# Attention tokens in transposed order, batch stores of 16 partitions, and another order of the first loads

## The chip, the cores and the metric

The kernel runs on one core of a Trainium2 chip. A core has five engines with a queue each: TensorE (PE, with weight loads shown as PEld), VectorE (DVE), ScalarE (ACT), GpSimd (POOL) and SyncE (SP, which here only issues transfers). Each queue runs in order; engines wait for each other by semaphores. Transfers between device memory and the on-chip memory run on 16 DMA engines and are issued from the queues of SP, ACT and POOL. The metric is the device time of one execution in microseconds (us).

## The reference

Two blocks follow each other. The inputs are q, k and v of 8 batches, 8 heads, 576 tokens, 64 numbers each, float32.

```
k_p = k.reshape(B, H, Sp, 8, D).mean(axis=3)          # 576 keys -> 72 pooled keys; v_p the same
scores = scale * q @ k_p^T ; attn = softmax(scores)
x = (attn @ v_p) as (B, S, H*D)                       # 8 x 576 x 512
s = x @ w_gate ; top_idx = the 128 tokens of a batch with the largest s
out = x ; out[top_idx] += sigmoid(s[top_idx]) * (relu(x[top_idx] @ w1) @ w2)   # 512 -> 1024 -> 512
```

Every token of x is written to the output; 128 tokens of each batch are then read back, sent through the two matrices w1 and w2, and written again.

## The kernel before

The work of a batch is cut into six *steps* of 96 tokens; there are 48 steps, numbered a = 0 to 47, and 14 more for what is left after the last attention. Two steps make a *unit* u.

The attention. k and q of a batch come as [128 partitions = 8 heads x 16 groups of 36 tokens]; v comes as [72 pooled rows] in two halves of four heads, each half as a transfer of 64 partitions and one of 8. `pool_k`, `k_trans` and `q_trans` build transposed operands, `pool_v` sums v over the pool of eight and multiplies it with the gate's weights, `gate_v` reduces that product to one column. `scores(u)` (L209) makes 32 matmuls into the PSUM tile pS and then one exponential on ACT (L220) for two steps at once: 72 partitions of 1536 numbers. The six token groups t and sixteen token groups g of a step lie in pS as (t g); the exponential writes them as (g t), so that consecutive results are six numbers apart. `attend(a)` (L226) makes the eight heads' matmuls into pA; `norm(a)` reads pA with two small ACT instructions (zall L244, ss L245) and two DVE instructions (rz L247, xs L248). pS and pA each have one buffer: `scores(u+1)` waits for the exponential of u, `attend(a+1)` for `norm(a)`.

The stores. After every second step ACT's queue issues a store of 96 partitions, two tokens each (L270), three per batch.

The second block of batch b is spread over later steps by a list of jobs: `at(a, slot, job)` puts a job into step a, slot 0 to 3. With e = 6(b+1), the first step of the next batch: `score` on DVE and POOL at e-1; `row_bcast` in two halves at e, slots 2 and 3: three transposes on PE into the tile pM, a copy by ACT (sr, L295), three more into the same pM, a copy. pM has one buffer, so PE's second three wait for ACT's first copy. Then come `count` and `one_hot` (DVE, steps e+2 to e+5), `gather` at e+6 (POOL issues the indirect read of 128 rows of the output, xr, L331, which waits for the stores of the batch), `x_trans` at e+7 slot 3 (PE, L346), `hidden` (L358) and `finish` (pF, L368, and POOL's indirect write, L374). So step e of a batch holds the first step of attention of the next batch, `row_bcast` of this one, `gather` of the one before it and part of `finish` of the one before that, and step e+1 ends with `x_trans`. I call the stretch from the second half of `attend(e)` to `x_trans` in e+1 the *boundary* at step e; boundaries with all their parts lie at steps 12, 18, 24, 30, 36 and 42.

The order of a step is written out: slot 0, `attend(a)`, `norm(a)`, slot 1, on even steps `scores(u+1)` and `q_trans(u+2)`, slots 2 and 3. PE, DVE, ACT and POOL run their parts in just that order.

The loads. SP issues k(b+2), q(b+2) and the two halves of v(b+2) during batch b, w1 at the start and w2 in step 3. v has three buffers (L101), k and q two. Load q(b+2) waits for the last `q_trans` of batch b, which stands in the first step of batch b+1.

One thing is not in the text of the kernel: the transfers that SP and ACT issue share eight completion semaphores, which the built program hands out in turn, over both queues together. Each transfer waits, at its place in its queue, until the transfer that had its semaphore before, eight transfers earlier, has landed. The list of waits in the built program names these.

At the end a check of all normalizers (L459 to L463) decides whether a second, general path is run; it isn't run here.

Of the kernel before, what the change touches and what calls it, by code (L numbers as in the profile page):

```python
# [7 lines left out]
FT = mybir.dt.float32  # L8
BF = mybir.dt.bfloat16
I32 = mybir.dt.int32  # L10
AF = mybir.ActivationFunctionType
# [37 lines left out]
def direct_path(ctx, tc, q, k, v, moe_w_gate, moe_w1, moe_w2, moe_capacity, out, flag):  # L49
# [49 lines left out]
        nc.sync.dma_start(out=QR[b], in_=q[b].rearrange("h (g t) d -> (h g) t d", g=G))  # L99

    def load_v(b, g, eng):  # L101
        x = work.tile([SP, HG, POOLW, D], FT, name="vraw", bufs=3)
        VR[b, g] = x
        src = v[b, HG * g : HG * (g + 1)].rearrange("h (p t) d -> p h (t d)", t=POOLW)
        for lo, hi in ((0, 64), (64, SP)):
            eng.dma_start(out=x[lo:hi].rearrange("p h t d -> p h (t d)"), in_=src[lo:hi])

    load_k(0)
    load_v(0, 0, nc.scalar)
    load_q(0)  # L110
    load_v(0, 1, nc.scalar)

# [2 lines left out]
                        in_=bass.AP(tensor=moe_w_gate.tensor, offset=moe_w_gate.offset, ap=[[0, SP], [1, DM]]))  # L117
    eps = const.tile([C, 1], FT)
    nc.vector.memset(eps, 1e-9 * POOLW)
    diff = const.tile([128, 128], FT)  # L120
    nc.gpsimd.iota(diff, pattern=[[1, 128]], base=0, channel_multiplier=-1,
                   allow_small_or_imprecise_dtypes=True)
# [21 lines left out]
    def constants():  # L144
        nc.vector.tensor_scalar(ident, diff, 0.0, None, op0=OP.is_equal)
        nc.vector.tensor_scalar(before, diff[:C, :C], 0.0, None, op0=OP.is_lt)
        nc.vector.memset(ones, 1.0)

        hi = const.tile([C, 1], FT, name="hi")
        stepped = const.tile([C, CT], FT, name="stepped")  # L150
        for t in range(CT):
            nc.vector.tensor_scalar(stepped[:, t : t + 1], part, float(G * (t + 1)), None, op0=OP.is_ge)
        nc.vector.tensor_reduce(out=hi, in_=stepped, axis=AX.X, op=OP.add)
        lo = const.tile([C, 1], FT, name="lo")
        nc.vector.scalar_tensor_tensor(lo, hi, -float(G), part, op0=OP.mult, op1=OP.add)
        nc.vector.tensor_scalar(lo, lo, float(NC), None, op0=OP.mult)
        nc.vector.tensor_scalar(hi, hi, float(NC * G), None, op0=OP.mult)
        for a in auxb:
            nc.vector.tensor_scalar(a[:, :, 0], chunk0, lo, None, op0=OP.add)
            nc.vector.tensor_scalar(a[:, :, 1], chunk0, 0.0, hi, op0=OP.mult, op1=OP.add)  # L160

# [2 lines left out]
    def pool_k(b, eng):  # L166
        x = KR[b].rearrange("p (r t) d -> p r t d", r=R)
        KS[b] = work.tile([128, R, D], FT, name="ks", bufs=1)
        eng.tensor_tensor(out=x[:, :, 0:2, :], in0=x[:, :, 0:2, :], in1=x[:, :, 2:4, :], op=OP.add)  # L169
        eng.tensor_tensor(out=KS[b], in0=x[:, :, 0, :], in1=x[:, :, 1, :], op=OP.add)  # L170
# [11 lines left out]
    def pool_v(b, g, eng):  # L182
        x = VR[b, g]
        VP[b] = vps[b % 2]
        h = slice(HG * g, HG * g + HG)
        eng.tensor_tensor(out=x[:, :, 0:4, :], in0=x[:, :, 0:4, :], in1=x[:, :, 4:8, :], op=OP.add)  # L186
        eng.tensor_tensor(out=x[:, :, 0:2, :], in0=x[:, :, 0:2, :], in1=x[:, :, 2:4, :], op=OP.add)  # L187
        eng.tensor_tensor(out=VP[b][:, h, 0:D], in0=x[:, :, 0, :], in1=x[:, :, 1, :], op=OP.add)

        eng.tensor_tensor(out=x[:, :, 2, :], in0=VP[b][:, h, 0:D], in1=wg[:, h, :], op=OP.mult)  # L190

    def gate_v(b, g):
        h = slice(HG * g, HG * g + HG)
        nc.vector.tensor_reduce(out=VP[b][:, h, D + 1], in_=VR[b, g][:, :, 2, :], axis=AX.X, op=OP.add)  # L194
# [5 lines left out]
    def q_trans(u):  # L200

        b, th = divmod(u, NTH)
        QT[u] = work.tile([128, 2, 2, CT, 32], FT, name="qt")
        nc.vector.transpose(  # L204
            out=QT[u].rearrange("p cc j t c -> p t (cc j) c"),
            in_=QR[b].rearrange("p (t c) d -> p t (c d)", c=NC)[:, :, 2 * D * th : 2 * D * (th + 1)].rearrange(
                "p t (a e) -> p t a e", e=32))

    def scores(u):  # L209
        b = u // NTH  # L210
        p = psum.tile([SP, 4, 4, 128], FT, name="pS")
        for s in range(2):
            for j in range(2):
                for i in range(4):
                    r = slice(32 * i, 32 * i + 32)
                    nc.tensor.matmul(p[:, i, 2 * s : 2 * s + 2, 0:C], KT[b][r, j, s, :],  # L216
                                     QT[u][r, :, j, :, G * s : G * s + G],
                                     start=(j == 0), stop=(j == 1))
        ET[u] = work.tile([SP, H * 2, G, CT], FT, name="et")
        nc.scalar.activation(ET[u].rearrange("p n g t -> p n t g"),  # L220
                             p.rearrange("p i n x -> p (i n) x")[:, :, 0:C].rearrange("p n (t g) -> p n t g", g=G),
                             AF.Exp, scale=exp_scale)

    PA = {}

    def attend(a):  # L226
        u, cc = divmod(a, 2)
        b = u // NTH
        p = psum.tile([C, 2, 512], FT, name="pA")
        for h in range(H):  # L230
            g, n = divmod(h, HG)
            nc.tensor.matmul(p[:, g, E * n : E * n + E], ET[u][:, 2 * h + cc].rearrange("p g t -> p (g t)"),  # L232
                             VP[b][:, h, :], start=True, stop=True)
        PA[a] = p[:, :, 0 : HG * E].rearrange("p g (n d) -> p g n d", d=E)

# [23 lines left out]
    def others(ins, b, kinds):  # L259
        for o in range(B):  # L260

            if o != b and not (kinds[-1] is gath and b == B - 1 and o == B - 2):
                for s in kinds:
                    for x in s.get(o, ()):
                        tc.declare_no_dep(ins.ins, x.ins, reason="rows of another batch")

    def store_x(u):
        b, th = divmod(u, NTH)
        c = slice(2 * th, 2 * th + 2)
        i = nc.scalar.dma_start(out=out[b].rearrange("(p c) d -> p c d", c=NC)[:, c, :], in_=XS[b][:, c, :])  # L270
        others(i, b, (scat, gath))
        store.setdefault(b, []).append(i)

    def score(b):
        nc.vector.tensor_tensor(out=SS[b], in0=SS[b], in1=RZ[b], op=OP.mult)
# [107 lines left out]
    def at(a, slot, *job):  # L383
        jobs.setdefault((a, slot), []).append(job)


    for u in range(NU):
        at(2 * u + 2, 1, store_x, u)
    for b in range(B):
        e = NC * (b + 1)  # L390
        last = b == B - 1
        at(e - 1, 3, score, b)
        at(e, 2, row_bcast, b, 0)
        at(e, 3, row_bcast, b, 1)
        for c in range(NC):
            at(e + (1 if last else (2, 2, 3, 3, 4, 5)[c]), 3, count, b, c)
        at(e + (2 if last else 5), 3, one_hot, b)
        at(e + (5 if last else 6), 3 if last else 1, gather, b)
        at(e + 7, 1, gate, b)
        at(e + 7, 3, x_trans, b)  # L400
        for n, f in enumerate((0, 1, 2, 3, 4, 5, 8, 6, 7, 9, 10, 11, 12, 13, 14, 15)):
            c = (0, 0, 1, 1, 2, 2, 2, 3, 3, 3, 4, 4, 4, 5, 5, 5)[n]
            slot = (1, 2, 1, 2, 1, 2, 2, 1, 2, 2, 1, 2, 2, 1, 2, 2)[n]
            at(e + 8 + c, slot, *((hidden, b, f) if f < 8 else (finish, b, f - 8)))
        if b + 1 < B:
            a = NC * b
            at(a, 0, pool_k, b + 1, nc.gpsimd)
            at(a + 1, 3, pool_v, b + 1, 0, nc.gpsimd)
            at(a + 2, 1, k_trans, b + 1)
            at(a + 3, 3, pool_v, b + 1, 1, nc.gpsimd)  # L410
            at(a + 4, 3, gate_v, b + 1, 0)
            at(a + 5, 3, gate_v, b + 1, 1)
        if b + 2 < B:
            at(a, 1, load_k, b + 2)
            at(a + 1, 1, load_q, b + 2)
            at(a + 2, 1, load_v, b + 2, 0, nc.sync)
            at(a + 4, 3, load_v, b + 2, 1, nc.sync)

    def run(a, slot):
        for f, *x in jobs.get((a, slot), ()):  # L420
            f(*x)

    pool_k(0, nc.vector)
    pool_v(0, 0, nc.gpsimd)
    k_trans(0)
    q_trans(0)
    scores(0)
    pool_v(0, 1, nc.vector)
    gate_v(0, 1)
    gate_v(0, 0)  # L430
    q_trans(1)
    load_k(1)
    for g in range(2):
        load_v(1, g, nc.sync)
    load_q(1)
    constants()
    nc.sync.dma_start(out=w1, in_=moe_w1.rearrange("(a p) f -> p a f", p=128))
    at(3, 1, lambda: nc.sync.dma_start(out=w2, in_=moe_w2.rearrange("(a p) n -> p a n", p=128)))

    for a in range(NCH + 14):  # L440
        run(a, 0)
        if a < NCH:
            attend(a)
            norm(a)
        run(a, 1)
        u = a // 2
        if a % 2 == 0 and u + 1 < NU:
            scores(u + 1)
            if u + 2 < NU:
                q_trans(u + 2)  # L450
        run(a, 2)
        run(a, 3)
# [367 lines left out]
```

## Time and profile before

| | |
|---|---|
| median of three executions | 365.19 us (364.87 to 366.78) |
| the profiled execution: time, span | 366.8 us, 364.9 us |
| mean granted TensorE clock | 0.865 of full speed |
| PE matmul busy | 275.2 us (75%) |
| DVE busy | 177.9 us (49%) |
| POOL busy | 134.5 us (37%) |
| ACT busy | 104.9 us (29%) |
| bytes moved | 46.75 MB, mean 128 GB/s |

The span is from the first to the last instruction of the profiled execution. An engine's busy time is the sum of its instructions' durations; issuing a transfer and waiting are not in it. The chain that ended last is followed back from the last instruction, at each step to what released it; PE has 44% of it, DVE 22%, transfers 16%, ACT 6%.

### The profile page before, as it was taken

How to read it: one execution, taken by the hardware profiler on the slowest of the kernel's cores; microseconds unless marked ns; L12 is line 12 of the kernel's file. 1: busy time of each engine (PE TensorE's matmuls, PEld its weight loads, DVE VectorE, ACT ScalarE, POOL GpSimd, SP SyncE). 2: the span in 40 equal slices, each digit the busy share in tenths (PEclk: the TensorE clock that was granted, in tenths of full speed). 3: DMA queues.
4: the chain of work that ended last, by engine and by line, in shares of the span. 5: the costliest groups of instructions: out<-in, count | busy, mean ns of one | idle time of the engine just before them, and what ended most of it. 6: DMA issues, size and time to landing. Idle time of an engine off the chain costs nothing.

```text
span 364.9 us, 5869 instructions
## 1 busy us (share of the span) xinstructions
PE 275.2 (75%) x2306; PEld 216.3 (59%) x2306; DVE 177.9 (49%) x524; ACT 104.9 (29%) x169; POOL 134.5 (37%) x156
## 2 busy tenths in 40 slices
PE   0303777788658988969778989698879889989890
PEld 0203666576637875767557755686668669556650
DVE  3249244158423752594429723946294627563001
ACT  0310333422240444324314441432343244110100
POOL 1177501950359015660647064805390210121101
PEclk9999766655565998988999998969996999999996
DMA  7932999961781178306661686031121113210101
GB/s 272 268 58 54 372 353 304 321 140 44 208 249 50 44 195 247 94 15 151 224 158 31 141 295 142 0 110 46 38 65 43 46 29 93 66 60 11 48 0 39
DMA packets 12952, 46.75 MB, mean 128 GB/s; under 512 B 1324, under 2 KB 1324, under 8 KB 10868
## 3 DMA queue, kind: packets, MB, share of 16 engines
q1 hardware_dynamic: 8240, 31.33, 29.4%
q10 hardware_dynamic: 3396, 10.77, 10.0%
q0 software_dynamic: 1280, 4.20, 4.2%
q8 instruction: 20, 0.33, 0.4%
q14 instruction: 16, 0.13, 0.1%
HBM read 34.75 MB, written 11.53 MB: 127 GB/s over the span
## 4 chain that ended last, share of the span: by engine, by line
PE 44%; DVE 22%; DMA 16%; ACT 6%; issue 5%; POOL 4%; ACTq 1%; DVEq 0%; SPq 0%; POOLq 0%
PE pA L232 14%; PE pM L358 10%; PE pS L216 8%; DMA xr<-out_dram,idx 8%; PE pF L368 8%; DMA vraw<-in_v_dram 7%; DVE xs L248 4%; ACT et L220 4%; DVE cmp L309 3%; POOL kraw L169 2%; DVE cmp L305 2%; DVE qt L204 2%; DVE cmp L307 2%; DVE oh L316 2%; DVE kh L175 2%
## 5 line engine op out<-in xcount | busy, mean ns | idle before, releaser
L232 PE MATMUL pA<-vp,et 72*96 72x66 f32 x768 | 90.8, 281 | 47.7 <-DVE vp L194 24.6
L232 PEld LDWEIGHTS pA<-vp,et 72*96 72x96 f32 x768 | 86.3, 195 | 59.0 <-issue 28.5
L220 ACT ACTIVATE et<-pS 72x1536 f32<-72x1536 f32 x24 | 70.7, 2947 | 61.9 <-PE pS L216 61.9
L358 PE MATMUL pM<-xg,w 128*128 128x128 f32 x512 | 71.3, 292 | 2.8 <-ACT xg L348 1.5
L358 PEld LDWEIGHTS pM<-xg,w 128*128 128x128 f32 x512 | 65.0, 203 | 8.7 <-issue 5.0
L368 PE MATMUL pF<-w,ht 128*128 128x512 f32 x128 | 65.2, 632 | 0.0
L247 DVE RECIPROCAL rz<-zall 96x8 f32<-96x8 f32 x48 | 9.5, 198 | 113.9 <-ACT zall L244 112.4
L216 PE MATMUL pS<-qt,kt 32*72 32x192 f32 x768 | 52.4, 428 | 12.0 <-DVE qt L204 12.0
L216 PEld LDWEIGHTS pS<-qt,kt 32*72 32x72 f32 x768 | 36.5, 184 | 19.4 <-DVE qt L204 12.0
L281 POOL CAST auxb<-sc 96x6 bf16<-96x6 f32 x8 | 1.6, 199 | 121.0 <-DVE sc L277 105.0
L186 POOL TENSOR_TENSOR vraw<-vraw 72x1024 f32<-72x1024 f32 x15 | 35.5, 2368 | 19.7 <-DMA vraw<-in_v_dram 19.6
L244 ACT ACTIVATE zall<-pA,eps 96x8 f32<-96x8 f32 x48 | 12.2, 254 | 93.8 <-PE pA L232 93.8
L248 DVE TENSOR_TENSOR xs<-pA,rz 96x512 f32<-96x512 f32 x48 | 33.0, 687 | 6.7 <-DVE rz L247 0.9
L368 PEld LDWEIGHTS pF<-w,ht 128*128 128x128 f32 x128 | 22.9, 200 | 17.9 <-issue 17.9
L307 DVE TENSOR_SCALAR_CACHE_REDUCE cmp<-sr,sc 96x576 bf16<-96x576 f32 (+5 forms) x48 | 26.6, 554 | 0.0
L204 DVE STREAM_TRANSPOSE qt<-qraw 128x768 f32<-128x768 f32 x24 | 23.2, 966 | 0.9 <-DMA qraw<-in_q_dram 0.9
L374 POOL DMA_INDIRECT out_dram<-y,idx x8 | 8.5, 1064 | 40.1 <-DVE y L373 22.0
L309 DVE SCALAR_TENSOR_TENSOR cmp<-sr,sc,before 96x96 bf16<-96x96 f32 x48 | 21.9, 456 | 0.3
L373 DVE SCALAR_TENSOR_TENSOR y<-pF,g,xr 128x512 f32<-128x512 f32 x8 | 6.0, 750 | 29.5 <-PE pF L368 29.5
L305 DVE TENSOR_SCALAR_CACHE_REDUCE cmp<-sr,sc 96x96 bf16<-96x96 f32 (+4 forms) x40 | 20.0, 499 | 0.7
L187 POOL TENSOR_TENSOR vraw<-vraw 72x512 f32<-72x512 f32 x15 | 19.1, 1277 | 1.2
L361 ACT ACTIVATE ht<-pM 128x512 f32<-128x512 f32 x16 | 9.6, 597 | 33.6 <-PE pM L358 33.6
(68 smaller groups left out, 182.4 us busy)
## 6 DMA issues: line engine op xcount, KB each, us to landing
kraw<-in_k_dram SPq DMA_DIRECT2D x8, 1152.0 KB
qraw<-in_q_dram SPq DMA_DIRECT2D x8, 1152.0 KB, 6.7
out_dram<-xs ACTq DMA_DIRECT2D x24, 384.0 KB, 3.0
vraw<-in_v_dram SPq DMA_DIRECT2D x14, 512.0 KB, 9.0
w<-in_moe_w_dram SPq DMA_DIRECT2D x2, 2048.0 KB, 27.3
vraw<-in_v_dram ACTq DMA_DIRECT2D x2, 512.0 KB, 19.9
vraw<-in_v_dram SPq DMA_DIRECT2D x14, 64.0 KB
wg<-in_moe_w_gate_dram ACTq DMA_DIRECT2D x1, 144.0 KB
```

The costliest lines, as they stand in the source:

```text
L186: eng.tensor_tensor(out=x[:, :, 0:4, :], in0=x[:, :, 0:4, :], in1=x[:, :, 4:8, :], op=OP.add)
L187: eng.tensor_tensor(out=x[:, :, 0:2, :], in0=x[:, :, 0:2, :], in1=x[:, :, 2:4, :], op=OP.add)
L204: nc.vector.transpose(out=QT[u].rearrange("p cc j t c -> p t (cc j) c"), in_=QR[b].rearrange("p (t c) d -> p t (c d)", c=NC)[:, :, 2 * D * ...
L216: nc.tensor.matmul(p[:, i, 2 * s : 2 * s + 2, 0:C], KT[b][r, j, s, :], QT[u][r, :, j, :, G * s : G * s + G], start=(j == 0), stop=(j == 1))
L220: nc.scalar.activation(ET[u].rearrange("p n g t -> p n t g"), p.rearrange("p i n x -> p (i n) x")[:, :, 0:C].rearrange("p n (t g) -> p n t ...
L232: nc.tensor.matmul(p[:, g, E * n : E * n + E], ET[u][:, 2 * h + cc].rearrange("p g t -> p (g t)"), VP[b][:, h, :], start=True, stop=True)
L248: nc.vector.tensor_tensor(out=XS[b][:, c, :].rearrange("p (g n d) -> p g n d", g=2, d=D), in0=o[:, :, :, 0:D], in1=rz.rearrange("p (g n on ...
L305: nc.vector.tensor_scalar(cmp[:, 0 : c * C], row[:, 0 : c * C], s, None, op0=OP.is_ge, op1=OP.add, accum_out=CN[b][:, c, 0:1])
L307: nc.vector.tensor_scalar(cmp[:, c * C : S], row[:, c * C : S], s, None, op0=OP.is_gt, op1=OP.add, accum_out=CN[b][:, c, 1:2])
L309: nc.vector.scalar_tensor_tensor(cmp[:, 0:C], row[:, c * C : c * C + C], s, before, op0=OP.is_equal, op1=OP.mult, accum_out=CN[b][:, c, 2:3])
L358: nc.tensor.matmul(p[:, f % 4, :], w1[:, d, 128 * f : 128 * f + 128], XG[b][:, d, :], start=(d == 0), stop=(d == DB - 1))
L368: nc.tensor.matmul(p, HT[b][:, f, :], w2[:, f, :], start=(f == 0), stop=(f == FB - 1))
```

## The change

- The exponential writes in the order in which it reads, (t g), so that its 96 results per head lie together. The tokens of a step then stand on the partitions in the order (t g) instead of (g t), and the two columns of token numbers (`auxb`) are computed for that order, with as many instructions as before.
- `store_x` runs once per batch, in slot 1 of step e, and issues six transfers from ACT's queue, one per token group t: 16 partitions, each with six consecutive tokens, 12 KB. There are 48 such stores instead of 24 of 96 partitions and 4 KB each.
- The first loads all go into SP's queue, in the order k0, half of v0, q0, other half of v0, k1, v1, q1, w1; before, ACT's queue issued v0 and the gate's weights while SP issued k0, q0, k1 and the rest. Only the gate's weights are left with ACT.
- ACT makes one small exponential at the very start, which brings the load of its function table there.
- `scores(1)` and `q_trans(2)` move ahead of the loop, and `constants`, `gate_v` and `pool_v` of batch 0 are reordered on DVE.
- v has four buffers instead of three.

The core of the diff:

```diff
-        x = work.tile([SP, HG, POOLW, D], FT, name="vraw", bufs=3)
+        x = work.tile([SP, HG, POOLW, D], FT, name="vraw", bufs=4)
...
     load_k(0)
-    load_v(0, 0, nc.scalar)
+    load_v(0, 0, nc.sync)
     load_q(0)
-    load_v(0, 1, nc.scalar)
+    load_v(0, 1, nc.sync)
...
+    nc.scalar.activation(const.tile([C, 1], FT, name="first"), eps, AF.Exp)
...
-        ET[u] = work.tile([SP, H * 2, G, CT], FT, name="et")
-        nc.scalar.activation(ET[u].rearrange("p n g t -> p n t g"),
-                             p.rearrange("p i n x -> p (i n) x")[:, :, 0:C].rearrange("p n (t g) -> p n t g", g=G),
-                             AF.Exp, scale=exp_scale)
+        ET[u] = work.tile([SP, H * 2, C], FT, name="et")
+        nc.scalar.activation(ET[u], p.rearrange("p i n x -> p (i n) x")[:, :, 0:C], AF.Exp, scale=exp_scale)
...
-    def store_x(u):
-        b, th = divmod(u, NTH)
-        c = slice(2 * th, 2 * th + 2)
-        i = nc.scalar.dma_start(out=out[b].rearrange("(p c) d -> p c d", c=NC)[:, c, :], in_=XS[b][:, c, :])
-        others(i, b, (scat, gath))
-        store.setdefault(b, []).append(i)
+    def store_x(b):
+        dst = out[b].rearrange("(g t c) d -> t g c d", g=G, c=NC)
+        store[b] = []
+        for t in range(CT):
+            i = nc.scalar.dma_start(out=dst[t], in_=XS[b][G * t : G * t + G, :, :])
+            others(i, b, (scat, gath))
+            store[b].append(i)
...
-    for u in range(NU):
-        at(2 * u + 2, 1, store_x, u)
     for b in range(B):
         e = NC * (b + 1)
+        at(e, 1, store_x, b)
...
+    load_k(1)
+    for g in range(2):
+        load_v(1, g, nc.sync)
+    load_q(1)
+    nc.sync.dma_start(out=w1, in_=moe_w1.rearrange("(a p) f -> p a f", p=128))
+    at(3, 1, lambda: nc.sync.dma_start(out=w2, in_=moe_w2.rearrange("(a p) n -> p a n", p=128)))
     pool_k(0, nc.vector)
     pool_v(0, 0, nc.gpsimd)
     k_trans(0)
     q_trans(0)
     scores(0)
+    q_trans(1)
+    scores(1)
+    constants()
+    gate_v(0, 0)
     pool_v(0, 1, nc.vector)
     gate_v(0, 1)
-    gate_v(0, 0)
-    q_trans(1)
...
+    q_trans(2)
...
-        if a % 2 == 0 and u + 1 < NU:
+        if a % 2 == 0 and 0 < u < NU - 1:
             scores(u + 1)
```

## The prediction

> **What bounds the kernel now.** I read the page's slices first (PE about 30% before 36 us, over 85% from 110 us on), then the windows by stage, then the timeline at the start and at one boundary, then the list of transfers.
>
> ```profile
> 0.00:33.00 33.00, 2.89 (x33) 1.95 (x33) 14.54 (x13) 4.21 (x2) 14.61 (x18) 1.00 0.60 165
> 33.00:62.00 29.00, 21.44 (x192) 18.12 (x192) 12.53 (x37) 9.96 (x15) 6.59 (x7) 0.76 0.98 326
> 62.00:97.50 35.50, 26.77 (x206) 22.67 (x206) 19.02 (x61) 10.83 (x17) 15.11 (x17) 0.55 0.66 175
> 188.30:210.40 22.10, 19.25 (x208) 17.08 (x208) 16.88 (x53) 8.77 (x13) 10.62 (x10) 1.00 0.38 94
> ```
>
> These windows give PE, PEld, DVE, ACT and POOL busy, the granted clock, the transfer share and GB/s. Until 33 us PE waits for loads; to 62 us the transfer engines are full (0.98); to 97.5 us PE runs at 0.55 of its clock; later it is 80 to 95% busy. The timeline of the start:
>
> ```profile
> 14.87 0.32 ACTq L116 DMA_DIRECT2D wg<-in_moe_w_gate_dram  x1
> 15.22 1.28 ACT L220 ACT_TABLE_LOAD   x1 [15.22 <-DMA vraw<-in_v_dram]
> 16.52 2.93 ACT L220 ACTIVATE et<-pS 72x1536 f32<-72x1536 f32 x1
> 23.14 1.22 DVE L186 TENSOR_TENSOR vraw<-vraw 72x1024 f32<-72x1024 f32 x1 [11.17 <-DMA vraw<-in_v_dram]
> 32.96 2.80 PE L232 MATMUL pA<-vp,et 72*96 72x66 f32 x16 [18.09 <-DVE vp L194]
> ```
>
> The first line matters most for the change: the gate's weights were ACT's fifth transfer, their semaphore had been v0's, and ACT stood from 3.5 to 14.87 us with everything behind it. A transfer that waits for its semaphore blocks its engine. Next, groups on ACT, and the boundary at step 18 (second half of its attention at 135.23, `x_trans` at 148.62, 13.4 us later):
>
> ```profile
> L220 ACT ACTIVATE et<-pS 72x1536 f32<-72x1536 f32 x24 | 70.7, 2947 | 61.9 <-PE pS L216 61.9
> L361 ACT ACTIVATE ht<-pM 128x512 f32<-128x512 f32 x16 | 9.6, 597 | 33.6 <-PE pM L358 33.6
> L295 ACT COPY sr<-pM 96x288 f32<-96x288 f32 x16 | 6.7, 418 | 8.0 <-PE pM L293 8.0
> ```
>
> ```profile
> 138.58 0.35 SPq L99 DMA_DIRECT2D qraw<-in_q_dram  x1
> 138.77 2.93 ACT L220 ACTIVATE et<-pS 72x1536 f32<-72x1536 f32 x1 [2.29 <-PE pS L216]
> 139.04 1.25 SPq L106 DMA_DIRECT2D vraw<-in_v_dram  x2
> 141.49 0.45 ACT L295 COPY sr<-pM 96x288 f32<-96x288 f32 x1
> 141.99 0.45 PE L293 MATMUL pM<-ident,sc 96*96 96x96 f32 x3 [1.19 <-ACT sr L295]
> 142.27 1.50 PE L232 MATMUL pA<-vp,et 72*96 72x66 f32 x16
> 143.61 4.49 PE L368 MATMUL pF<-w,ht 128*128 128x512 f32 x6
> 148.62 0.63 PE L346 MATMUL pM<-ident,xr 128*128 128x128 f32 x4 [0.52 <-DMA xr<-out_dram,idx]
> ```
>
> PE's second transposes wait for ACT's copy, which stands behind the exponential; whatever holds ACT here holds PE. The loads of q and v start 3.4 and 3.8 us into the boundary, and the list of transfers (last column: issue to landing) says when they land:
>
> ```profile
> qraw<-in_q_dram SPq DMA_DIRECT2D x8, 1152.0 KB, 6.7
> out_dram<-xs ACTq DMA_DIRECT2D x24, 384.0 KB, 3.0
> vraw<-in_v_dram SPq DMA_DIRECT2D x14, 512.0 KB, 9.0
> ```
>
> **The change part by part.**
>
> *The exponential* (24). Two contiguous rows, 597 ns for 512 numbers and 418 for 288, give 0.80 ns a number and 0.19 us fixed, so 1.42 us for 1536; I take 1.46. The upper end is today's 2.95, if the order of writing isn't the cause. That frees 36 us of ACT, but the chain holds only 4.0% (14.6 us, five instances), nearly all before 100 us.
>
> *The start.* In one queue k0, half of v0, q0, half of v0 are 3.7 MB with the gate's weights; at 326 GB/s behind 2.3 us of dead time that is 13.6 us, at the 200 GB/s seen where v runs (below) for its part 15 us. v0 landed at 23.1. DVE has by then transposed q and made the constants (2.1 us) and starts `pool_v` at 16.8. It cost 8.8 us because POOL worked beside it (L187 took 3.62 there; 1.22 for the larger L186 alone); alone about 2.6. POOL's `pool_k(1)` starts about 18.5, so I take 3.8; with `gate_v` the first attention is at 21 (19.8 to 26) instead of 32.96. The table load (1.28) lies beside the loads.
>
> *Steps 0 to 7.* Attention alone took 9.8 us per two steps (42.48 to 52.27): 2.83 attend, 2.85 scores, 2.93 exponential over the other attend, 1.1 norm. With 1.46 the attend (1.75) is longer, so 8.6. Steps 0 and 1 have no scores left and take 7.5. Step 6 starts at 44.5 (62.13 before). There the first batch's six stores stand on ACT ahead of the next exponential, and the built program's waits name, in turn, two pieces of v1, w1, q2, a piece of v2, and w2. w2 ends 14.4 MB of loads; with 1 MB of stores, at 326 GB/s and 2.3 + 1 us, it lands at 50. Then exponential, copy, transposes, attend at half clock and norm: step 8 at 56.7 instead of 74.75, a gain of 18. A warmer clock wins nothing here, w2 decides.
>
> *Steps 8 to 12.* 8 to 10 took 10.0 with DVE last (`k_trans`, `q_trans`, `count`): as before. 10 to 12 takes 8.6 for 9.9. Gain 1.3 (to 6 if PE gets its full clock). Sum so far: 19.3.
>
> *The boundaries.* The store takes six places in ACT's queue between zall and the exponential. Six issues cost 1.9 us (0.32 each), hidden while PE makes scores. The waits do not hide. At step 18 the built program's last store waits for v(5)'s first half, and at 12 and 24 for v(4)'s and v(6)'s: loads that SP issues *in this same boundary*, after `q_trans`. At 30 the fifth waits for q7. Behind ACT stand the exponential, both copies, PE's transposes and all of PE. Working for 18, from the boundary's start: v issued +3.8, 9.0 to land, 0.7 for larger stores ahead: +13.5; store issue 0.3, exponential 1.46, copy 0.45, transposes 0.5: attend at +16.3, at half clock 2.83, pF 4.49: `x_trans` at +23.6 instead of +13.4. Loss 10.2; at 24, for 13.0 before, 10.6. At 12, v at +14, no pF: +19.5 for 13.5, 6.0. At 30, q7 lands at 3.4 + 6.7 + 0.7 = +10.8: +20.9 for 13.3, 7.6. Together 34.4. The gather (7.7 us from 140.8) is covered by this stall. At 36 and 42 no load is left: the copy comes 1.5 earlier, or the gather 2 later beside a threefold store; I take -0.5 each. Bound below: if the load lands by +3.4, nothing is lost; above, as follows.
>
> *Stores of 16 partitions.* The trace has none. A piece is 0.2 MB: 0.5 us at q's rate, 128 partitions; v's 64 partitions ran at half that:
>
> ```profile
> 141.00:143.00 2.00, 1.01 (x12) 1.01 (x13) 0.00 (x0) 1.33 (x3) 0.88 (x1) 1.00 0.97 389
> 145.00:147.00 2.00, 2.00 (x4) 0.74 (x3) 0.19 (x2) 0.00 (x0) 0.00 (x0) 0.50 0.96 178
> ```
>
> (last column; q fills the first window, v and the gather the second). Scaling on to 16 gives 45 GB/s, 4 us a piece. In the sum I take the q end, as the pieces' packets are large like q's (9 KB, v's are 2 KB) and neighbouring pieces lie on other partitions. With the geometric middle, 1.4 us, the five pieces ahead of v take 7 us instead of 2.5: 4.5 more at each of four boundaries, 18. With 4 us, one after another, it would be 17 each; I give that 1 in 50.
>
> Here a rule of the Trainium skill speaks against the change: "SBUF — State Buffer", Door 1, says a transfer reaches only the ports of its partitions, 16 partitions four of sixteen, about 104 GB/s. The two windows agree for 64 against 128 (178 to 389 GB/s). By the page's figure a piece takes 1.9 us and five 9.5, 7 more at each boundary; the sum would be about 407 (an estimate from that page).
>
> *Four v buffers, moved loads, the rest.* SP waited 132 us in all for v's buffer (DVE vp), but after the start only 4.5 us of waiting for v reached an engine, on POOL, hidden. So no gain; v's second half and k now follow q and v into the boundary, behind them. Between boundaries the step that waits has DVE last; I take -2 (0 to -9, six times 1.5). At step 48 the last store, 1.2 MB at once, runs beside the gather of batch 6, issued 318.8 and needed at 322.4: +2 (0 to 4). Token columns: same instructions.
>
> **Sum.** -19.3 + 34.4 - 1 - 2 + 2 = +14.1 on the profiled execution's 366.8 us (span 364.9 and 1.9 around it). That run is 1.6 above the median; on the median 365.2 it gives 379.
>
> **Rivals.**
> - *Faster: ACT's wait ends early.* One mechanism: the loads the stores wait for land sooner. It decides at a loss of 5.1 a boundary (20.3 over four) for 8.6, an unlock 3.5 us earlier (v 5.5 us after issue, not 9.0). For it: one q landed after 5.7. Against: v follows a q of 1.2 MB and landed after 9.0 where seen. Without any wait: 365 - 19 - 3 + 2 = 345; half-way 358.
> - *Much slower: 16-partition stores crawl.* Four boundaries 2.5 to 4.5 us more: 389 to 397, and a tail above.
> - *The change doesn't do what it says: the exponential stays at 2.95.* Adds 1.5 at four boundaries and 2.5 before: 387. Against: both contiguous rows.
> - *No matter:* the gains and losses cancel, 363.4 to 367.
>
> **How the numbers follow.** Forecast 0.55 (367 to 388; the start can be 5 later, steps 8 to 12 5 better, a boundary 2 either way), faster 0.20, crawling stores 0.13, slow exponential 0.06, no matter 0.06. The predicted time is 379. The range 356 to 398 leaves out about 0.13 of the faster case below and 0.06 above. Within 0.5% (1.8 us, about what a measurement can tell): 0.06. Faster by more 0.20, slower by more 0.74.
>
> **What would show it.** The exponential's group at 1.4 to 1.5 us; the first attend near 21; step 8 near 57. In ACT's waits, transfers of v, q and w2 ahead of et, about 8 to 10 us at four boundaries; PE's wait for sr up from 11.8 to some 40 us, half clock behind it; boundaries of 20 to 24 us until 30, and 11 after. If ACT shows no such wait, the forecast is wrong and the time is near 345; if the store's landing grows past 6 us, the second rival is at work.

## The result, and where the time went

The changed kernel takes 415.9 us (median of 4 executions, 407.1 to 419.1); the kernel before took 365.0 us beside it. The ratio is 1.122, with a 95% interval of 1.107 to 1.137. So it is slower, as forecast, but by 51 us and not by 14: 379 was predicted, with a range up to 398. The ratio leaves out executions more than 1.5% above the fastest of their kernel, here the two of 418.9 and 419.1 (the profiled one), so it is smaller than that of the medians (1.139), and the profile below holds some 9 us more than the ratio counts.

The profiled execution took 419.1 us with a span of 417.3, 52.4 more than the span of before. The same instants of both traces, in us (a boundary runs from the second half of `attend(e)` to `x_trans` in e+1):

| stretch | before | after | difference | predicted |
|---|---|---|---|---|
| start to the second half of attend(12) | 97.51 | 90.09 | -7.4 | -19.3 |
| boundary at 12 | 13.5 | 24.3 | +10.7 | +6.0 |
| boundary at 18 | 13.4 | 28.8 | +15.4 | +10.2 |
| boundary at 24 | 13.1 | 27.7 | +14.7 | +10.6 |
| boundary at 30 | 13.3 | 25.9 | +12.6 | +7.6 |
| boundaries at 36 and 42 | 22.0 | 30.6 | +8.6 | -1.0 |
| the five stretches between boundaries | 125.7 | 122.6 | -3.1 | -2 |
| from x_trans after step 42 to the end | 66.4 | 67.3 | +0.9 | +2 |

The forecast's sum was +14.1, the stretches add up to +52.4. Of the 38.3 us between, 19.0 are the four boundaries at 12 to 30, 11.9 the start and 9.6 the boundaries at 36 and 42; the rest came out 2.2 lower.

The groups on the page of after (busy time and mean ns of one; then idle time of the engine before them and what ended it):

```profile
L222 ACT ACTIVATE et<-pS 72x1536 f32<-72x1536 f32 x24 | 34.7, 1447 | 148.8 <-PE pS L218 62.5
L294 PE MATMUL pM<-ident,sc 96*96 96x96 f32 x48 | 8.8, 305 | 69.3 <-ACT sr L296 69.3
```

The exponential is 1.45 us, half of before. And PE stands 69.3 us for ACT's copy sr, 11.8 before: that is the whole loss and more, at one place. What holds ACT there is in its waits (total us, times, longest):

```profile
ACT et L222 <- DMA vraw<-in_v_dram: 53.3, 3, 17.9
...
ACT et L222 <- DMA out_dram<-xs: 17.9, 3, 6.9
ACT et L222 <- issue: 15.1, 1, 15.1
```

The first line is the three boundaries at 12, 18 and 24, the last the one at 30, the one between them step 6 and the boundaries at 36 and 42. "Issue" at 30 means that this view finds no cause; the view of the tile that q is loaded into has it, among those that waited for it:

```profile
  ACT et L222: 15.1, 1
```

The timeline of the boundary at 18, the same that was shown of before (start us, duration, and in brackets the idle time and what ended it):

```profile
139.34 0.89 PE L232 MATMUL pA<-vp,et 72*96 72x66 f32 x8 [1.03 <-DVE vp L196]
140.33 0.32 ACTq L271 DMA_DIRECT2D out_dram<-xs  x1
140.70 17.73 ACTq L271 DMA_DIRECT2D out_dram<-xs  x5
...
143.10 0.35 SPq L99 DMA_DIRECT2D qraw<-in_q_dram  x1
143.54 4.43 SPq L106 DMA_DIRECT2D vraw<-in_v_dram  x4
144.90 1.06 POOL L332 DMA_INDIRECT xr<-out_dram,idx  x1 [0.28 <-POOL idx L328]
...
158.52 1.45 ACT L222 ACTIVATE et<-pS 72x1536 f32<-72x1536 f32 x1 [17.93 <-DMA vraw<-in_v_dram]
...
160.82 2.72 PE L232 MATMUL pA<-vp,et 72*96 72x66 f32 x16
...
168.13 0.60 PE L347 MATMUL pM<-ident,xr 128*128 128x128 f32 x4
```

The six issues of the store stretch over 18 us; the last one goes at 158.10, when v, issued at 143.54 in the same boundary, has landed 14.6 us later; only then come the exponential, PE's attention (granted clock 0.50, 2.72 us for 1.50) and 7 us later `x_trans`. That is the chain the prediction wrote down, with one number wrong: it let v land 9.7 us after its issue. The list of transfers (last column: median us from issue to landing) says the same of all loads:

```profile
qraw<-in_q_dram SPq DMA_DIRECT2D x8, 1152.0 KB, 13.4
...
vraw<-in_v_dram SPq DMA_DIRECT2D x16, 512.0 KB, 14.5
```

q took 6.7 and v 9.0 before. And one place was not in the prediction at all: at steps 36 and 42 no load is left, every transfer that a piece would have to wait for is of an earlier batch and long done, and still the timeline at 36 has

```profile
295.98 0.32 ACTq L271 DMA_DIRECT2D out_dram<-xs  x1
296.34 5.54 ACTq L271 DMA_DIRECT2D out_dram<-xs  x5
...
301.98 1.45 ACT L222 ACTIVATE et<-pS 72x1536 f32<-72x1536 f32 x1 [5.75 <-DMA out_dram<-xs]
```

Six issues take 5.9 us, where 0.32 each had been taken: they start at 295.98, 296.34, 296.81, 297.97, 299.04 and 300.11, so that from the third on they come about every 1.07 us.

At the start the first attention is at 24.40 us (32.96 before, 21 predicted) and step 8 at 67.36 (74.75 before, 56.7 predicted).

Three questions follow. Is it the place of the store in ACT's queue, or the slow transfers? What makes v's landing 5 us longer? And what became of the gain at the start?

### The profile page after: what moved, and what is told of

It is laid out like the page before. It is cut to its first block, busy times and chain, and to the rows that moved or that the text cites. A ratio compares the mean times of both kernels' runs of the same rounds, so it can differ in the third digit from the quotient of the medians.

```text
span 417.3 us, 5895 instructions
## 1 busy us (share of the span) xinstructions
PE 289.4 (69%) x2306; PEld 225.7 (54%) x2306; DVE 172.6 (41%) x524; ACT 72.1 (17%) x170; POOL 133.2 (32%) x156
## 4 chain that ended last, share of the span: by engine, by line
PE 44%; DVE 20%; DMA 19%; issue 5%; ACTq 4%; ACT 4%; POOL 2%; SPq 1%; DVEq 0%; POOLq 0%
PE pA L232 18%; DMA vraw<-in_v_dram 11%; PE pF L369 10%; PE pM L359 8%; PE pS L218 6%; DMA qraw<-in_q_dram 6%; DVE xs L248 4%; ACTq L271 4%; DVE cmp L310 3%; DVE qt L206 2%; DVE kh L177 2%; DVE oh L317 2%; DVE cmp L306 2%; DVE cmp L308 1%; ACT zall L244 1%
## 5 line engine op out<-in xcount | busy, mean ns | idle before, releaser
L232 PE MATMUL pA<-vp,et 72*96 72x66 f32 x768 | 97.4, 294 | 27.5 <-DVE xs L248 19.5
L232 PEld LDWEIGHTS pA<-vp,et 72*96 72x96 f32 x768 | 92.8, 208 | 39.1 <-DVE xs L248 20.3
L369 PE MATMUL pF<-w,ht 128*128 128x512 f32 x128 | 71.7, 686 | 0.0
L218 PE MATMUL pS<-qt,kt 32*72 32x192 f32 x768 | 55.1, 445 | 18.8 <-DVE qt L206 17.2
L359 PEld LDWEIGHTS pM<-xg,w 128*128 128x128 f32 x512 | 62.9, 198 | 8.6 <-issue 4.9
L222 ACT ACTIVATE et<-pS 72x1536 f32<-72x1536 f32 x24 | 34.7, 1447 | 148.8 <-PE pS L218 62.5
L294 PE MATMUL pM<-ident,sc 96*96 96x96 f32 x48 | 8.8, 305 | 69.3 <-ACT sr L296 69.3
L218 PEld LDWEIGHTS pS<-qt,kt 32*72 32x72 f32 x768 | 38.2, 194 | 27.5 <-DVE qt L206 17.2
L294 PEld LDWEIGHTS pM<-ident,sc 96*96 96x96 f32 x48 | 5.5, 149 | 75.5 <-ACT sr L296 71.1
L188 POOL TENSOR_TENSOR vraw<-vraw 72x1024 f32<-72x1024 f32 x15 | 35.3, 2352 | 13.7 <-DMA vraw<-in_v_dram 13.4
L369 PEld LDWEIGHTS pF<-w,ht 128*128 128x128 f32 x128 | 25.3, 220 | 20.8 <-issue 20.8
L244 ACT ACTIVATE zall<-pA,eps 96x8 f32<-96x8 f32 x48 | 12.6, 263 | 103.0 <-PE pA L232 103.0
L171 POOL TENSOR_TENSOR kraw<-kraw 128x1152 f32<-128x1152 f32 x7 | 18.3, 2617 | 7.6 <-DMA kraw<-in_k_dram 7.6
## 6 DMA issues: line engine op xcount, KB each, us to landing
kraw<-in_k_dram SPq DMA_DIRECT2D x8, 1152.0 KB, 15.5
qraw<-in_q_dram SPq DMA_DIRECT2D x8, 1152.0 KB, 13.4
vraw<-in_v_dram SPq DMA_DIRECT2D x16, 512.0 KB, 14.5
```

What stands on the lines that cost most here:

```text
L222: nc.scalar.activation(ET[u], p.rearrange("p i n x -> p (i n) x")[:, :, 0:C], AF.Exp, scale=exp_scale)
L244: nc.scalar.activation(z.rearrange("p (g n) -> p g n", g=2), o[:, :, :, D], AF.Identity, bias=eps)
L359: nc.tensor.matmul(p[:, f % 4, :], w1[:, d, 128 * f : 128 * f + 128], XG[b][:, d, :], start=(d == 0), stop=(d == DB - 1))
L369: nc.tensor.matmul(p, HT[b][:, f, :], w2[:, f, :], start=(f == 0), stop=(f == FB - 1))
```

## Experiments: who stands at the store

The fifteen runs are numbered as they ran; a text of what was expected speaks of earlier ones by these numbers. The first four are the changed kernel with one edit each.

**Run 4: the stores issued by SP.**

```diff
-            i = nc.scalar.dma_start(out=dst[t], in_=XS[b][G * t : G * t + G, :, :])
+            i = nc.sync.dma_start(out=dst[t], in_=XS[b][G * t : G * t + G, :, :])
```

> The changed kernel with its six pieces of 16 partitions issued by SP in place of ACT; result as the reference's. ACT can't stand at the store then. Waits theory: ACT's exponential follows the scores at once, PE's wait for sr (69 us) nearly goes; the gather comes late instead (six pieces at 1.07 us, landing 4.4, gather 5 to 8: x_trans 17 to 20 us into the boundary for 25 to 29): 370 to 388 us. If slow transfers alone carry it: x_trans as late as now, time over 400.

354.5 us (351.1 to 355.5), ratio to the kernel before 0.973 [0.962, 0.985]. One word takes 61 us away (54 by the ratios). The boundary at 18:

```profile
119.80 0.89 PE L232 MATMUL pA<-vp,et 72*96 72x66 f32 x8 [1.03 <-DVE vp L196]
...
123.34 1.45 ACT L222 ACTIVATE et<-pS 72x1536 f32<-72x1536 f32 x1 [2.29 <-PE pS L218]
125.36 1.06 POOL L332 DMA_INDIRECT xr<-out_dram,idx  x1 [0.28 <-POOL idx L328]
...
126.14 1.50 PE L232 MATMUL pA<-vp,et 72*96 72x66 f32 x16
...
136.45 1.09 PE L347 MATMUL pM<-ident,xr 128*128 128x128 f32 x4 [6.18 <-DMA xr<-out_dram,idx]
```

The exponential follows the scores at once, the attention runs at full clock, and PE now waits for the gather: 16.7 us for 28.8. I had expected the gather later, and 370 to 388 us. So the same 16-partition pieces cost little when no computing engine stands at them: with three v buffers, in runs 11 and 14 below, 6 us over the store of before.

**Run 2: sixteen partitions that lie apart.** The built program has the same order of transfers and the same waits as the changed kernel; only the rows that a piece reads differ.

```diff
-in_=XS[b][G * t : G * t + G, :, :]
+in_=XS[b][t::CT, :, :]
```

> The changed kernel, each of the six pieces read from 16 partitions that lie six apart (t, t+6, ...) in place of 16 neighbours; same bytes, same place in ACT's queue, same waits in the built program (rows of x land at other places of out). Theory A1 (16 neighbouring partitions make a slow transfer): at steps 36 and 42, where no load runs, the six issues go from 5.9 and 5.4 us back to about 2; v's landing goes from 14.5 to about 9 us, the four earlier boundaries shrink by about 5 us each, and the time is 380 to 390 us. Theory A2 (16 partitions are slow wherever they lie, or 1.2 MB beside the loads is too much): no change, 407 to 419 us.

393.2 us (391.3 to 400.5), ratio to the kernel before 1.080 [1.069, 1.091]. 23 us of the loss by the medians, 15 by the ratios, are the neighbourhood of the partitions. The store's queue on the page (packets, MB, share of 16 engines' span), of after:

```profile
q10 hardware_dynamic: 1620, 9.59, 11.0%
```

and of this run, with as many packets and bytes:

```profile
q10 hardware_dynamic: 1620, 9.59, 7.4%
```

Over 417.3 and 398.6 us and 16 engines that is 453 and 291 ns a packet. The boundary at 18 of this run:

```profile
140.85 2.62 SPq L106 DMA_DIRECT2D vraw<-in_v_dram  x4
...
151.70 1.45 ACT L222 ACTIVATE et<-pS 72x1536 f32<-72x1536 f32 x1 [13.40 <-DMA vraw<-in_v_dram]
```

The last piece goes at 151.08, 10.2 us after v's issue, for 14.6. The boundaries at 12 to 30 are 20.7, 24.2, 24.3 and 22.3 us; the prediction, which had left slow pieces out of its sum, had 19.5, 23.6, 23.6 and 20.9. Those at 36 and 42 are 13.5 and 13.4, about half-way back: the six issues still take 4.7 and 4.5 us there, where I had expected 2. (In the next run, with 96 partitions a piece, they take 2.8 and 3.9.)

Here the page "SBUF — State Buffer" of the Trainium skill, section Door 1, which the prediction weighed and did not take, points the right way: it gives a transfer of 16 neighbouring partitions four of sixteen ports and about 104 GB/s. The runs agree that neighbours are slow; the estimate worked out from the page, 7 us more a boundary, lies above the 4.1 to 5.2 measured. They don't show the figure: at step 36 a piece of 192 KB was issued every 1.07 us, which is 184 GB/s. That pieces on other partitions overlap may be why; no run shows it.

**Run 3: six pieces of 96 partitions.**

```diff
-        for t in range(CT):
-            i = nc.scalar.dma_start(out=dst[t], in_=XS[b][G * t : G * t + G, :, :])
+        for t in range(NC):
+            i = nc.scalar.dma_start(out=dst[:, t, :], in_=XS[b][:, t, :])
```

> The changed kernel, its store cut the other way: six pieces of 96 partitions and one chunk each (2 KB a partition for 12 KB), same bytes and same place (rows of x land at other places of out). The program's shared semaphores fall differently: ACT's pieces then wait for loads of a boundary earlier, not for those of the same boundary. If the waits for the same boundary's loads carry the loss: no wait of ACT for v, boundaries of 11 to 15 us, time 350 to 365. If the amount stored at once carries it, whoever waits: boundaries of 18 us and more, time over 385.

351.6 us (350.6 to 355.0), ratio 0.969 [0.958, 0.981]. No wait of ACT for v is left; the six issues at 18 take 3.7 us and the boundary 14.5. From run 2 to this one 42 us went: here the pieces differ (96 partitions, 2 KB each) and the semaphores fall on older loads, so this run alone doesn't divide the two. Together the three say that the store's place in ACT's queue is worth 54 to 61 us (by the ratios and by the medians), and that spreading the partitions alone takes back 15 to 23 of them.

## Experiments: what the fourth v buffer does

**Run 1: all of the change but the store.**

```diff
...
+        i = nc.scalar.dma_start(out=out[b].rearrange("(p c) d -> p c d", c=NC)[:, c, :], in_=XS[b][:, c, :])
...
+    for u in range(NU):
+        at(2 * u + 2, 1, store_x, u)
...
-        at(e, 1, store_x, b)
```

> The changed kernel with the store of the kernel before: one transfer of 96 partitions and two chunks after every second step, in place of six transfers of 16 partitions at the batch's end (rows of x land at other places of out, so out isn't the reference's). Theory A (the batch store is what costs, by ACT's waits at it and by its slow transfers): boundaries back to the 11 to 13.5 us of the kernel before, step 8 not later than 60 us, time 345 to 358 us. Theory B (the moved loads and four v buffers collide at the boundaries, the store only shows the delay): boundaries stay over 20 us and the time over 390.

359.7 us (354.4 to 361.9), ratio 0.980 [0.974, 0.987], neither the one nor the other: boundaries of 17.5, 18.4 and 15.7 us at 18, 24 and 30, shorter than 25 to 29, longer than the 13.1 to 13.4 of before, and step 8 at 60.9. Something besides the store makes boundaries longer.

**Run 9: the fourth buffer alone**, in the kernel before.

```diff
-        x = work.tile([SP, HG, POOLW, D], FT, name="vraw", bufs=3)
+        x = work.tile([SP, HG, POOLW, D], FT, name="vraw", bufs=4)
```

> The kernel before with a fourth v buffer and nothing else. Theory (the loads moved ahead cost): SP no longer waits for a buffer, so the second half of v and k are issued at the boundary just ahead of the gather, the gather lands some 12 us after its issue in place of 7.7, and x_trans comes 2 to 4 us later at steps 18, 24 and 30; part of it is won back where loads would have come later: 368 to 376. Rival (more buffers do no harm): 363 to 367.

378.0 us (374.9 to 380.8), ratio 1.042 [1.034, 1.049]: one more buffer costs 12.5 us, and PE's wait for xr goes from 6.2 to 21.2 us. The boundary at 18:

```profile
137.82 0.89 PE L232 MATMUL pA<-vp,et 72*96 72x66 f32 x8 [1.02 <-DVE vp L194]
...
141.17 0.35 SPq L99 DMA_DIRECT2D qraw<-in_q_dram  x1
141.62 2.49 SPq L106 DMA_DIRECT2D vraw<-in_v_dram  x4
143.40 1.07 POOL L331 DMA_INDIRECT xr<-out_dram,idx  x1 [0.28 <-POOL idx L327]
144.20 0.35 SPq L95 DMA_DIRECT2D kraw<-in_k_dram  x1
...
154.84 1.09 PE L346 MATMUL pM<-ident,xr 128*128 128x128 f32 x4 [5.84 <-DMA xr<-out_dram,idx]
```

Before, SP issued q and one half of v here (two v transfers) and then stood until a buffer came free; the other half and k went out 9 us before the next boundary (166.56 and 167.76), long before its gather. With four buffers q, all of v and k, 3.5 MB, are under way with the gather of 128 rows, for which PE waits until 11.4 us after its issue, for 7.8, and the boundary takes 17.0 us for 13.4. SP's 132 us of waiting had kept these loads out of the gather's way.

**Runs 5 and 10: the first loads, with four and with three buffers.** The kernel before with the new order of loads and preparations and the early table load; exponential, tokens and store as before. From run 5 to run 10:

```diff
-        x = work.tile([SP, HG, POOLW, D], FT, name="vraw", bufs=4)
+        x = work.tile([SP, HG, POOLW, D], FT, name="vraw", bufs=3)
```

> The kernel before with only the other order of the first loads and of the preparations, the early table load and the fourth v buffer; exponential, token order and store as before. Together with the first run (359.7 us, which has the contiguous exponential too): if the exponential is worth what the steps said (about 1.2 us in each of the three or four pairs of steps of the start, little elsewhere) this takes 363 to 367, so the start alone wins nothing to speak of; rival: the start carries the whole gain and the exponential none: 358 to 361. First attend between 21 and 25 in both.

> The fifth run (start, early table load, four v buffers: 365.1) with three v buffers. If the fourth buffer is what gives the start's gain back at steps 18 to 30: boundaries of 13 to 14 us there again for 15 to 17.5, and 354 to 360. If the gain goes elsewhere (a clock that falls, loads that are late anyway): 363 to 367.

365.1 us (362.5 to 368.7; ratio 1.0005 [0.996, 1.005]) with four and 355.9 us (352.5 to 358.7; ratio 0.979 [0.971, 0.986]) with three. The first is 9 us ahead at step 8 (65.63 for 74.75), 5 at `x_trans` after step 18, and 0.2 after step 30: the gain of the start is real and is given back in boundaries of 17.5, 17.2 and 15.2 us. With three buffers those are 12.8, 13.0 and 12.8, and 9.6 us remain. So run 5 met its 363 to 367, but not for the reason given, that the start wins nothing.

**Runs 13 and 14: the square.** Two more corners, by the same edit: the changed kernel with three buffers, and run 1 with three.

> The changed kernel with three v buffers; result as the reference's. Theory (the fourth buffer brings v and k of two batches on into the boundary itself, so that ACT's last stores wait for loads that have just been issued): with three, the built program's last pieces wait for v and k that SP issued before the boundary; ACT's wait falls from 15 to 18 us to the 6 to 9 us of the slow pieces, and the time to 376 to 392 us. Rival (ACT waits as long whatever the buffers): over 405.

> The first run (all but the store: 359.7 us) with three v buffers: start and exponential alone (rows of x land at other places of out). If the parts add up (365.4 less 9.6 for the start with three buffers, less 7.3 for the exponential): 346 to 351. If the fourth buffer does no harm once the exponential is short: 357 to 362.

| start and exponential of after | store of before | six pieces on ACT | cost of the store |
|---|---|---|---|
| three v buffers | 344.6 (340.6 to 348.5) | 367.9 (363.3 to 372.4) | 23 |
| four v buffers | 359.7 (354.4 to 361.9) | 415.9 (407.1 to 419.1) | 56 |
| cost of the buffer | 15 | 48 | |

The two costs don't add: together they take 71 us, where 23 and 15 make 38. The remaining 33 us are the meeting of the two. (By the ratios, 0.942, 1.007, 0.980 and 1.122 of 365 us, the store costs 24 and 52, the buffer 14 and 42, and 28 are left for the meeting.) Where they lie is shown by the waits on ACT of the changed kernel with three buffers, 43 us for transfers ahead of the exponential where the changed kernel has 86:

```profile
ACT et L222 <- DMA out_dram<-xs: 30.8, 6, 5.4
ACT et L222 <- DMA w<-in_moe_w_dram: 11.8, 1, 11.8
```

No v and no q is in them. In the built program its pieces wait for loads that SP issued before the boundary, and the last one for its own first piece; what is left is 5.4 us and less. (The second line is step 6, where the last piece waits for w2.) I had expected 376 to 392. It is 8 us better: its boundaries at 18, 24 and 30 are 14.5, 15.5 and 15.1 us, those of run 12, from which the expectation was made, 18.5, 17.2 and 16.7.

**Run 12: the store alone**, six pieces on ACT in the kernel before, three buffers and the long exponential.

```diff
...
+            i = nc.scalar.dma_start(out=dst[t], in_=XS[b][G * t : G * t + G, :, :])
...
-    for u in range(NU):
-        at(2 * u + 2, 1, store_x, u)
...
+        at(e, 1, store_x, b)
```

> The kernel before with only the batch's store by six pieces of 16 partitions on ACT (rows of x land at other places of out). Here the program's waits let the last pieces of steps 12 to 30 wait for k(b+3), which SP issues ahead of the boundary, not in it. Waits theory: only the slow transfers are left, 4 to 6 us at each of six boundaries and step 6: 385 to 402. If the store costs the same whatever ACT waits for: 410 and more.

396.3 us (395.1 to 397.3), ratio 1.094 [1.087, 1.101], as expected without a wait for loads of the same boundary:

```profile
145.86 5.81 ACTq L271 DMA_DIRECT2D out_dram<-xs  x5
...
151.77 2.89 ACT L220 ACTIVATE et<-pS 72x1536 f32<-72x1536 f32 x1 [6.01 <-DMA out_dram<-xs]
...
155.46 2.72 PE L232 MATMUL pA<-vp,et 72*96 72x66 f32 x16
```

## Experiments: the exponential, and a better kernel

**Run 6: the contiguous exponential alone** in the kernel before.

```diff
-        nc.scalar.activation(ET[u].rearrange("p n g t -> p n t g"),
...
+        nc.scalar.activation(ET[u], p.rearrange("p i n x -> p (i n) x")[:, :, 0:C], AF.Exp, scale=exp_scale)
```

> The kernel before with only the contiguous exponential (tokens then lie in transposed order, and rows of x land at other places of out). The step said 36 us of ACT freed but only five instances on the chain, nearly all before 100 us: a gain of 3 to 8 us, 357 to 362. Rival: ACT's earlier copies shorten all boundaries by 1.5: 350 to 355. Rival: another engine is last at once: 363 to 366.

358.1 us (353.6 to 360.6), ratio 0.973 [0.960, 0.985]: 7.3 us for 36 us of ACT, inside the 3 to 8 expected. The place is another: of the 8.7 us between the two profiled spans only 3.4 lie ahead of the second half of `attend(12)` (94.09 us for 97.51), where the step had put nearly all.

**Runs 7 and 8: tokens ordered on PE.** They put the tokens in order on PE, which reads the scores' columns with g outside and t inside; the store is six pieces of one chunk on ACT as in run 3, or one transfer by SP. Four v buffers in both.

```diff
-                                     QT[u][r, :, j, :, G * s : G * s + G],
+                                     QT[u][r, :, j, :, G * s : G * s + G].rearrange("p c t g -> p c g t"),
...
+            i = nc.sync.dma_start(out=dst, in_=XS[b])
```

> The changed kernel with the tokens put in their order on PE, in place of ACT or the store: the scores' matmuls read their 96 columns with g outside and t inside, so the exponential stays contiguous and a partition holds six rows of out in order; six stores of 96 partitions, one chunk each, on ACT. Result as the reference's. If PE reads the columns 128 bytes apart at no cost: the scores' group stays at 445 ns a matmul and the time at that of the third run, 350 to 355. If the stride costs PE: over 600 ns a matmul, 365 to 385.

> As the run with the tokens ordered on PE, but the batch stored by one transfer of 96 partitions, 12 KB each, issued by SP. Result as the reference's. ACT never waits for a transfer; SP issues one transfer in place of six. Expected a little below the fourth run (354.5): 346 to 354, with x_trans 12 to 15 us into the boundary. If one transfer of 1.2 MB lands later than six pieces did: 354 to 362.

358.2 us (356.2 to 365.3; ratio 0.979 [0.970, 0.988]) and 365.0 us (362.2 to 367.9; ratio 1.002 [0.997, 1.007]). The stride isn't free; the group of the first of them, and that of run 3, which has the same store without the stride:

```profile
L218 PE MATMUL pS<-qt,kt 32*72 32x192 f32 x768 | 68.6, 506 | 17.6 <-DVE qt L206 16.0
...
L218 PE MATMUL pS<-qt,kt 32*72 32x192 f32 x768 | 52.6, 429 | 17.5 <-DVE qt L206 16.0
```

A matmul takes 506 ns for 429, at a mean granted clock of 0.859 for 0.841, so the clock isn't why; the group takes 16 us more and the kernel 6.6 (358.2 for 351.6). Run 7 falls between its two expectations. Run 8 misses its own: PE's wait for xr is 18.1 us in it, 10.9 in the first. That the single transfer is the reason was not separated.

**Run 11: stores on SP and three buffers.**

```diff
-        x = work.tile([SP, HG, POOLW, D], FT, name="vraw", bufs=4)
+        x = work.tile([SP, HG, POOLW, D], FT, name="vraw", bufs=3)
...
-            i = nc.scalar.dma_start(out=dst[t], in_=XS[b][G * t : G * t + G, :, :])
+            i = nc.sync.dma_start(out=dst[t], in_=XS[b][G * t : G * t + G, :, :])
```

> The changed kernel with the stores on SP (fourth run, 354.5) and three v buffers; result as the reference's. If the fourth buffer costs here as well: 345 to 352. If SP's stores then wait behind loads that wait for a buffer, and the gather with them: 356 to 370.

350.6 us (342.9 to 352.0); the kernel before beside it 365.5 (360.2 to 368.3). All its times lie below all of before's. Of the kernels that leave every row in its place it has the lowest median (run 4, with four buffers, 354.5): 15 us under the kernel before, 65 under the changed one.

**Run 15: the tokens ordered by the store**, two chunks after every second step in one transfer of 96 partitions, the rows of out counted t outside and g inside; three buffers.

```diff
...
+        i = nc.scalar.dma_start(out=out[b].rearrange("(g t c) d -> t g c d", g=G, c=NC)[:, :, c, :],
+                                in_=XS[b][:, c, :])
...
```

> The last kernel (start and contiguous exponential, three v buffers, a store of two chunks after every second step) with its tokens put in their places by the store itself: one transfer from 96 partitions, whose rows of out are counted t outside, g inside. Result as the reference's. If the order of the rows in out costs nothing (4 KB a row as before): 341 to 349 us, as the last one. If a transfer with two strides of rows is cut into slow pieces, as the six were: 355 and more.

357.9 us (353.4 to 360.2), ratio 0.978 [0.971, 0.985], 13 us over run 14 with its plain rows (344.6). The store's issues (duration ns min/median/max) in this run,

```profile
L270 ACTq DMA_DIRECT2D out_dram<-xs x24: 734/743/857, 37.4 to 307.8; - x24
```

and in the one with plain rows:

```profile
L270 ACTq DMA_DIRECT2D out_dram<-xs x24: 322/323/344, 36.0 to 295.0; - x24
```

An issue of 0.74 us is not 13 us; PE's wait for xr went from 11.1 to 19.2 us, and why the gather lands later was not followed up.

## Why the prediction was right or wrong

- *Direction and mechanism: right.* The store stands in ACT's queue and waits for a load of the same boundary, behind it the exponential, sr, PE's transposes. The views named for it show it: ACT's waits for v and q at four boundaries, PE's wait for sr at 69 us (some 40 forecast), half clock behind it; and taking the stores off ACT removes 54 to 61 us. What failed is the size of three terms: the pieces, their issues, and the rate of the first loads.
- *"Stores of 16 partitions": wrong, the largest miss.* The step took "the q end", 0.5 us a piece, and put the crawl into a rival with 0.13. Measured are 1.07 us a piece where no load runs, and v landing 14.6 us after its issue for the 9.7 of the step. That is 4 to 5 us at each of four boundaries, 19 in all, the 18 of its own geometric middle (1.4 us a piece); with the partitions spread (run 2) the forecast boundaries are met within 1.4 us. That it is mostly the neighbourhood, and not the number of partitions, run 2 shows. The row for v, 64 partitions at half of q's rate, stood in the text and was the nearest in kind; the size of the packets was a weak reason against it.
- *"Six issues cost 1.9 us (0.32 each), hidden": wrong.* They take 5.5 and 5.9 us even without a wait for a load, and those boundaries cost 8.6 us more than before, where the step had -1.
- *"Four v buffers": "no gain" is wrong.* Alone the fourth buffer costs 12.5 us. (The -2 of that step stood for the stretches between boundaries, and -3.1 was measured there.) The step saw that SP's wait reached no engine and that v's second half and k would follow into the boundary, and then looked only at what was gained. What these loads make late is the gather. The claim that the stall covers the gather holds in the changed kernel (PE waits there for the gather in no boundary); but the stall itself needs the fourth buffer: with three the pieces don't wait for this boundary's loads at all, which the step on the boundaries took as given.
- *"Start", "steps 0 to 7": right in kind, 10.7 us off at step 8.* First attend 24.4 for 21; over the runs with this order it lies between 21.0 and 26.0. Step 6 comes at 50.9 for 44.5; the step's own parts, 21, 7.5 and twice 8.6, give 45.7. That w2 decides is right: w2 is issued at 33.38, lands 27.1 us later, and the sixth piece, which waits for it, goes at 60.52:

```profile
60.52 0.32 ACTq L271 DMA_DIRECT2D out_dram<-xs  x1
60.94 1.45 ACT L222 ACTIVATE et<-pS 72x1536 f32<-72x1536 f32 x1 [6.87 <-DMA out_dram<-xs]
```

(The bracket names one of the store's own pieces, which were landing at that time.) From there it is 6.8 us to step 8, for the 6.7 of the step. What failed is w2's landing at 50, which took 15.4 MB at 326 GB/s. The window to 60.5 us, with columns as in the prediction, has the transfer engines full and 257 GB/s:

```profile
0.00:60.50 60.50, 32.65 (x275) 26.88 (x275) 23.18 (x54) 9.44 (x20) 28.72 (x34) 0.84 1.01 257
```

Why these loads ran slower than those from 33 to 62 us of before was not tested. In run 1, with the store of before and so no wait of ACT for w2, step 8 is at 60.9, 6.5 us earlier, of which 2.1 are there at the first attend already; so some 4 of the 10.7 us go with the store.
- *Exponential: right in size.* 1.45 us, and worth 7.3 alone; but less than half of that came before 100 us.
- *Steps 8 to 12: wrong, small.* 22.73 us for 22.76 before, -1.3 forecast.
- *Sum of the gains: met, in part by luck.* Start and exponential with three buffers and the store of before (run 14) give -20.9; the steps had -19.3. But they put all of it ahead of the second half of `attend(12)`, where run 14 has 14.2.
- *Tail:* +0.9 for +2.

The rivals: no sign of an early end of ACT's wait (its half-way time, 358, is 362 by its own numbers), and the exponential did shorten. The crawling stores came true on top of the forecast, as their 389 to 397 had it, with 4.1 to 5.2 us more at each of four boundaries for 2.5 to 4.5. The sign named for them, a store's landing past 6 us, does not show in the median (4.8 us), only in the longest (9.7).

## What to carry to other kernels

Issue stores from a queue that does nothing else: on a computing engine each issue can wait for an unrelated transfer's semaphore, or simply for the pieces ahead of it. Before a buffer is added, ask where the wait that it removes had been keeping transfers; a load that comes earlier can collide with one that is needed. And when two costs meet in one stretch, test the corners: here 23 and 15 us made 71 by the medians.

## What was not expected of the hardware

- An issue is not always short: 0.32 us alone, about 1.07 us each from the third on when pieces of 16 neighbouring partitions follow each other, with no load to wait for. The page "Perfetto Trace Analysis" of the Trainium skill, section "DMA Instruction — HWDGE (DVE, Sync)", says that the time recorded for an issue includes waiting for the shared descriptor generator and using it; the runs agree that it stretches, but don't show what it waits for.
- Sixteen partitions six apart move a packet in 291 ns, sixteen neighbours in 453 ns, with the same packets and order.
- PE reads columns 128 bytes apart more slowly: 506 ns a matmul (run 7) for 429 (run 3).
